# The first load of an elementwise kernel, split by rows into 4 and 60

## Chip, cores, metric

One core of one Trainium2 chip. The metric is the device time of a whole execution in microseconds. Times are medians of several runs; a ratio is the mean time of one kernel's fast runs over the mean of the other's fast runs in the same rounds, so it is not quite the ratio of the medians.

## The reference

```python
B, S, D = 1024, 16, 512          # bf16
def reference(x, y, gamma):      # x, y: (B, S, D); gamma: (D,)
    return x + gamma * y
```

16.8 MB each of x and y are read, and 16.8 MB are written. Seen by 128 partitions, each has 128 rows of 1 KB.

## The kernel before

It is written as lists of transfers. SP loads y and x, ACT loads gamma and stores, VectorE multiplies in place in `y_sb` and then adds x. `x_sb` has room for 75 rows only, so the second x load (rows 64 to 116, the fourth transfer of SP) has to wait for the addition of the first 53 rows. The start barriers are the point at which the engines wait for each other before the program proper; `EARLY` says how many transfers are issued ahead of it.

```python
PIECES = [53, 11, 53, 11]        # rows of one VectorE instruction
SP  = [('y', 0, 64), ('x', 0, 64, 0), ('y', 64, 128), ('x', 64, 117, 0), ('x', 117, 128, 64)]
ACT = [('g',), ('s', 0, 64), ('s', 64, 128)]
EARLY = (1, 0)                   # so many transfers of SP, of ACT, ahead of the start barriers
RELEASE = ('x', 64, 117, 0)      # the stores may start once this load has landed
DVE = [('m', 0), ('m', 1), ('a', 0), ('a', 1), ('m', 2), ('m', 3), ('a', 2), ('a', 3)]
# ... (cut)
            elif kind == "y":
                r = slice(w[1], w[2])
                i = eng.dma_start(out=y_sb[:, r, :], in_=yv[:, r, :]).then_inc(s_load[w], 16)
# ... (cut)
    for kind, *args in DVE:
        c = args[0]
        yt = y_sb[:, starts[c] : starts[c + 1], :]
        if kind == "m":
            need(y_loads, c)     # waits for every y load that meets the piece
            g = gamma_sb[:, None, :].to_broadcast([P, PIECES[c], D])
            nc.vector.tensor_tensor(out=yt, in0=yt, in1=g, op=MULT).then_inc(s_dve, 1)
```

Of the kernel before, what the change touches and what calls it, by code (L numbers as in the profile page):

```python
# [6 lines left out]



SP = [('y', 0, 64), ('x', 0, 64, 0), ('y', 64, 128), ('x', 64, 117, 0), ('x', 117, 128, 64)]  # L10
ACT = [('g',), ('s', 0, 64), ('s', 64, 128)]

EARLY = (1, 0)


RELEASE = ('x', 64, 117, 0)
# [11 lines left out]
def kernel(  # L28
# [30 lines left out]
    y_sb = nc.alloc_sbuf_tensor("y_sb", [P, rows, D], dt).ap()  # L59
    x_loads = [w for w in SP + ACT if w[0] == "x"]  # L60
    y_loads = [w for w in SP + ACT if w[0] == "y"]
    stores = [w for w in SP + ACT if w[0] == "s"]
    for loads in (x_loads, y_loads, stores):
# [32 lines left out]
    def ring(eng, what, n_early):  # L96

        known, went = 0, False
        for k, w in enumerate(what):
            kind = w[0]  # L100
            need = frees(w) if kind == "x" else pieces_of(w[1], w[2]) + list(w[3:]) if kind == "s" else []
            need = max((order[c] + 1 for c in need), default=0)
            if kind == "s" and not went:
                _take(s_go, 1, eng)
                went = True
            if need > known:
                eng.wait_ge(s_add, need)
                known = need
            if kind == "g":
                i = eng.dma_start(out=gamma_row, in_=gamma.unsqueeze(0)).then_inc(s_gamma, 16)  # L110
            elif kind == "x":
                to = x_sb[:, w[3] : w[3] + w[2] - w[1], :]
                i = eng.dma_start(out=to, in_=xv[:, w[1] : w[2], :]).then_inc(s_load[w], 16)
# [3 lines that stand above are left out]
            else:  # L117
                r = slice(w[1], w[2])
                i = eng.dma_start(out=ov[:, r, :], in_=y_sb[:, r, :]).then_inc(s_out, 16)
            if k < n_early:  # L120
                early.append(i.ins)

    ring(nc.sync, SP, EARLY[0])
    ring(nc.scalar, ACT, EARLY[1])

# [84 lines left out]
```

## Time and profile before

| | before |
|---|---|
| time, us (before the change was run) | 120.16 (119.85 to 120.28, 3 runs) |
| span of the profile | 118.6 us |
| VectorE busy | 70.0 us, 59% |
| the two DMA queues | 66.0% + 32.6% of 16 engines |

How to read it: VectorE is idle for two fifths of the span, and the DMA engines for 1.4%. Each DMA engine takes one packet after another; a load gives each of the 16 engines 8 packets and one small packet for the semaphore, the counter by which a waiting engine learns that the data has landed (the 720 packets of q1 are 5 loads of 128 + 16). The lines are in the prediction below. Its packet times come from the trace's record of every DMA packet (start, length, bytes, queue), which the printed page only sums up.

### The profile page before, as it was taken

To read this page: it belongs to the slowest core of one execution; us is meant where nothing else is said; L and a number is where in the kernel's file an instruction comes from. 1 tells how busy PE (TensorE), PEld (TensorE's weight loads), DVE (VectorE), ACT (ScalarE), POOL (GpSimd) and SP (SyncE) were. 2 spreads that over 40 slices of the span, in tenths; PEclk is the share of its full clock that TensorE was granted. 3 is DMA by queue.
4 is the path that set the end of the run, shared out by engine and by line. 5 is a ranking of instruction groups with operands and counts; after the bars stand their busy time and mean duration, and the time that the engine had idled before them with its cause. 6 is when DMAs were issued, how large, how long until landed. Compare 5 with 4: busy or idle time off the path is not lost. (4 is left out here: it accounts for less than half of the span.)

```text
span 118.6 us, 78 instructions
## 1 busy us (share of the span) xinstructions
PE 0.6 (0%) x1; PEld 0.1 (0%) x1; DVE 70.0 (59%) x10; POOL 0.2 (0%) x4
## 2 busy tenths in 40 slices
PE   0001000000000000000000000000000000000000
PEld 0000000000000000000000000000000000000000
DVE  0002000599999299999759999999999910000000
POOL 0000000000000000000000000000000000000000
DMA  9889888998899888998896969598899888988892
GB/s 354 354 376 685 354 354 354 597 464 354 354 398 663 354 354 354 663 398 354 354 586 293 586 293 567 220 639 354 354 575 486 354 354 376 685 354 354 354 619 88
DMA packets 1010, 50.33 MB, mean 424 GB/s; under 512 B 113, under 2 KB 114, under 8 KB 114
## 3 DMA queue, kind: packets, MB, share of 16 engines
q1 hardware_dynamic: 720, 33.55, 66.0%
q10 hardware_dynamic: 290, 16.78, 32.6%
HBM read 33.56 MB, written 16.78 MB: 424 GB/s over the span
## 5 line engine op out<-in xcount | busy, mean ns | idle before, releaser
L156 DVE TENSOR_TENSOR y_sb<-y_sb,gamma_sb 128x27136 bf16<-128x27136 bf16 (+1 forms) x4 | 34.6, 8688 | 12.7 <-DVEq L25 12.7
L165 DVE TENSOR_TENSOR y_sb<-x_sb,y_sb 128x27136 bf16<-128x27136 bf16 (+1 forms) x4 | 34.6, 8688 | 2.3 <-DVEq L25 2.2
L132 DVE CAST gamma_sb<-gamma_ps 128x512 bf16<-128x512 f32 x1 | 0.7, 692 | 8.8 <-DVEq L25 8.8
L127 DVE MEMSET ones_row<- 1x128 bf16 x1 | 0.2, 165 | 1.5 <-PEq L41 1.5
L130 PE MATMUL gamma_ps<-gamma_row,ones_row 1*128 1x512 bf16 x1 | 0.6, 578 | 9.7 <-PEq L25 9.7
L130 PEld LDWEIGHTS gamma_ps<-gamma_row,ones_row 1*128 1x128 bf16 x1 | 0.1, 100 | 9.7 <-issue 9.7
L194 POOL MEMSET const-uint8-127<- 128x1 uint8 x1 | 0.1, 102 | 0.0
L194 POOL MEMSET const-bfloat16-1.0<- 128x1 bf16 x1 | 0.1, 101 | 0.0
L194 POOL MEMSET const-float32-0.0<- 128x1 f32 x1 | 0.1, 98 | 0.2 <-issue 0.2
L194 POOL MEMSET const-float32-1.0<- 128x1 f32 x1 | 0.1, 98 | 0.0
## 6 DMA issues: line engine op xcount, KB each, us to landing
x_sb<-in_x_dram SPq DMA_DIRECT2D x1, 6784.0 KB, 20.8
x_sb<-in_x_dram SPq DMA_DIRECT2D x1, 1408.0 KB, 23.9
y_sb<-in_y_dram SPq DMA_DIRECT2D x2, 40.2
out_dram<-y_sb ACTq DMA_DIRECT2D x2, 22.8
x_sb<-in_x_dram SPq DMA_DIRECT2D x1, 39.7
gamma_row<-in_gamma_dram ACTq DMA_DIRECT2D x1, 1.0 KB
```

The lines of the kernel that those rows point to most:

```text
L127: nc.vector.memset(ones_row, 1.0).then_inc(s_ones, 1)
L130: nc.tensor.matmul(gamma_ps, ones_row, gamma_row, start=True, stop=True).then_inc(s_ps, 1)
L132: nc.vector.tensor_copy(out=gamma_sb, in_=gamma_ps).then_inc(s_dve, 1)
L156: nc.vector.tensor_tensor(out=yt, in0=yt, in1=g, op=MULT).then_inc(s_dve, 1)
L165: nc.vector.tensor_tensor(out=yt, in0=xt, in1=yt, op=ADD).then_inc(s_add, 1)
L194: nc = _bacc.Bacc("TRN2", target_bir_lowering=False, num_devices=1)
```

## The change

The intent is to let a small piece of the first load through first. The 4 rows and the other 60 are two transfers with two semaphores, both ahead of the barriers.

```diff
-SP = [('y', 0, 64), ('x', 0, 64, 0), ('y', 64, 128), ('x', 64, 117, 0), ('x', 117, 128, 64)]
+SP = [('y', 0, 4), ('y', 4, 64), ('x', 0, 64, 0), ('y', 64, 128), ('x', 64, 117, 0), ('x', 117, 128, 64)]
-EARLY = (1, 0)
+EARLY = (2, 0)
```

## The prediction

> **What bounds the kernel now.** I read the engine table first, then the DMA lines of the page, then the waits, then the order of time, and last the single packets in the trace. The page:
>
> ```profile
> span 118.6 us, 78 instructions
> PE 0.6 (0%) x1; PEld 0.1 (0%) x1; DVE 70.0 (59%) x10; POOL 0.2 (0%) x4
> DMA  9889888998899888998896969598899888988892
> ...
> q1 hardware_dynamic: 720, 33.55, 66.0%
> q10 hardware_dynamic: 290, 16.78, 32.6%
> HBM read 33.56 MB, written 16.78 MB: 424 GB/s over the span
> ```
>
> VectorE works 59% of the span, so no compute engine is the bound. The two DMA queues (q1 carries the loads issued by SP, q10 gamma and the stores issued by ACT) together hold 66.0 + 32.6 = 98.6% of the time of the 16 DMA engines. Only 1.4% of 118.6 us, about 1.7 us, is DMA time not filled. The digits of 8 and 9 are not idleness: a packet is counted in the slice in which it starts. Whatever this change does must come out of those 1.7 us, or be added to the rest.
>
> Who waits on the compute side:
>
> ```profile
> DVE y_sb L156 <- DVEq L25: 12.7, 2, 10.8
> DVE gamma_sb L132 <- DVEq L25: 8.8, 1, 8.8
> DVE y_sb L165 <- DVEq L25: 2.2, 1, 2.2
> ```
>
> These are VectorE's waits for loads: 10.8 us for the first y, 2.2 us for x, about 1.9 us for the second y. The data sets the pace. The order of time (start us, length us, what):
>
> ```profile
> 0.00 0.37 SPq L116 DMA_DIRECT2D y_sb<-in_y_dram  x1
> ...
> 1.43 0.33 SPq L113 DMA_DIRECT2D x_sb<-in_x_dram  x1
> 1.43 0.52 ACTq L110 DMA_DIRECT2D gamma_row<-in_gamma_dram  x1
> ...
> 9.70 0.10 PEld L130 LDWEIGHTS gamma_ps<-gamma_row,ones_row 1*128 1x128 bf16 x1 [9.70 <-issue]
> ...
> 10.46 0.69 DVE L132 CAST gamma_sb<-gamma_ps 128x512 bf16<-128x512 f32 x1 [8.78 <-DVEq L25]
> 21.94 17.29 DVE L156 TENSOR_TENSOR y_sb<-y_sb,gamma_sb 128x27136 bf16<-128x27136 bf16 x2 [10.79 <-DVEq L25]
> ...
> 76.88 18.86 ACTq L119 DMA_DIRECT2D out_dram<-y_sb  x2
> ```
>
> The first y load is issued ahead of the start barriers, at 0.00. The other queues start at 1.43, after the barriers. The first multiplication starts at 21.94.
>
> The packet records of the trace complete this. One packet is one partition's contiguous piece: 64 rows are 65,536 B and take 2.418 us when the engine was already busy, which is 27.1 GB/s for an engine and 434 GB/s for 16. Following the records, all 16 engines have a packet in hand at every moment from about 1.6 us to 117.6 us. The first packets start between 1.00 and 1.63 us, take 2.70 to 3.40 us (mean 3.11) and end between 4.04 and 4.55 us. The last engine writes its last semaphore packet at 118.22 us, the first at 117.64. So the span is a start, a stream and a tail:
> - an engine's stream, 40 packets of 2.418, 8 of 2.004 (53 rows) and 8 of 0.42 us (11 rows): 96.7 + 16.0 + 3.4 = 116.1 us;
> - ahead of it, for the last engine, 4.55 - 2.42 = 2.13 us. For a mean engine this is 1.90: about 1.21 until its first packet starts, and 0.69 by which that packet is longer than a warm one;
> - after it about 0.36 us to the end of the span.
>
> 2.13 + 116.1 + 0.36 = 118.6. The time of a run, 120.16, is some 1.5 us more than the span, outside what the change touches.
>
> **What the Trainium skill says.** "DMA: Bandwidth & Descriptors", section "Where 436 GB/s comes from", puts the ceiling of the 16 engines' ports at 435 GB/s; the packets' 434 agree, so the stream is at its ceiling. The same page, section "Latency and other measured facts", gives about 600 ns to the first byte of a DMA issued from SP or ACT. The trace has 0.63 us between the end of the issue (0.37) and the first packet's start (1.00): agreed, if that is what is meant. The page's section "Why a DMA increments its semaphore by 16 and not by 1" says that each engine's last descriptor writes the semaphore; the trace has 16 landings for the first y load, from 21.33 to 21.81 us. "Perfetto Trace Analysis", section "DMA Optimizations", says that splitting DMAs may let some start sooner and helps "If DMA engines are generally idle". Here they are idle only before 1.6 us.
>
> **The change part by part.** In the instruction streams, SP gets one transfer more (4 rows, then 60, both ahead of the barriers), and the first multiplication waits for two semaphores instead of one. Nothing else moves.
>
> 1. More packets. 128 packets of 65,536 B become 128 of 4,096 and 128 of 61,440 B: 8 more for each engine. The fixed part of a packet comes from two sizes: (2004 - 422) ns / (54272 - 11264) B is 36.8 ps a byte, and 422 ns less 11264 x 36.8 ps leaves about 8 ns. 8 x 8 = 64 ns, and one more semaphore packet of 9 ns: about +0.07 us in the stream, fully on the path, since the engines are never idle.
>
> 2. A later barrier. SP's second early issue takes as long as its other issues, 0.33 to 0.45 us, so x and gamma are issued at about 1.85 instead of 1.43. x is not reached in the ring before 20.9 us, so it doesn't count. gamma_sb is ready at about 11.2 us and wanted at 21.94: ten microseconds to spare. It may even land earlier, because it now comes behind short packets instead of 64 KB ones (its 1 KB packet ran at 6.82 us, at the end of a round of large ones). Either way: 0.
>
> 3. The second wait of the multiplication. It still needs all 64 rows, because the piece is 53 rows and the tail of the load comes last. Nothing is multiplied earlier. The semaphore already there is taken within about 0.1 us (21.83 to 21.94 is such a step), and VectorE's lead over the stores (the second store is issued at 95.4, the first one lands until 99.3) absorbs it: 0.
>
> 4. The start. The first transfer has the same 128 descriptors and the same issue, so its first packets should start at the same 1.00 to 1.63 us. Then 8 packets of 158 ns by the fit, 1.26 us in all, cover an engine until about 3.2 us, with the latency of the first. The second transfer, issued some 0.4 us after the first, should have its descriptors there by 1.4 to 2.1 us. So no hole is expected. Whether anything is gained depends on the 0.69 us: a plain latency from the first read to the first write stays as it is with 4 KB.
>
> Sum: +0.07 us if the latency is a constant; 120.16 becomes 120.2.
>
> **The rivals.** *Short packets start faster.* Four cold 8 KB packets of the runtime, before the kernel, took 0.49 to 0.57 us against 0.31 for two others, an excess of about 0.2 to 0.26, not 0.69. If the excess grows with the packet, because something of it is read before the first write, up to 0.69 - 0.24 = 0.45 us is saved: 119.8 with part 1. Against it: 16 engines starting together may be what makes 0.69, and the last engine to start had an excess of only 0.28 with the same 64 KB. I give this one chance in three. *A hole between the two transfers.* If the second transfer's descriptors come late, as a fresh start of about 1 us rather than behind the first, every engine stands still for up to 0.5 us: 120.7. The early issue speaks against it: one in ten. *The early y rows or gamma let VectorE begin earlier.* This would move only VectorE, which is not the bound, and the multiplication needs row 52 anyway: nothing. *A shift in the spread of the engines.* The slowest engine sets the end, and the engines' starts lie 0.5 us apart; another order may move the end by 0.2 us either way.
>
> **Range and chances.** Two parts in three at 120.2, a third at 119.8 with some holes above: 120.1. The three runs of before lie from 119.85 to 120.28 by themselves, and the effects are at most half a microsecond, so 119.6 to 120.5 should hold 8 times in 10. 2% is 2.4 us. A gain of that size is more than the whole 1.7 us of unfilled DMA time, so faster gets 0.01; slower by 2.4 us would need a hole in the stream that nothing in the trace suggests: 0.01.
>
> **What would show it right or wrong.** The profile after should have a span of 118.2 to 118.9 us, q1 with 720 + 128 + 16 = 864 packets, the second multiplication wait without length, VectorE's first multiplication again at about 22 us, and x's issue near 1.85. The first 4 KB packets should start at 1.0 to 1.6; if the latency is constant, the engines pass their first 64 KB at 4.1 to 4.6 as before, and if the first rival is right, at about 3.7 to 4.1. A gap between the end of the eighth short packet and the start of the first 60 KB packet is the second rival. A time outside of the range would mean that the stream itself changed its rate, for instance packets of 61,440 B slower than 2.27 us, or that a later transfer was issued too late.

## The result, and the profile after

120.06 us (119.92 to 120.14, 6 runs) against 120.09 us (119.85 to 120.28, 6 runs). The ratio is 0.9998, 95% interval 0.9985 to 1.0011: no difference that these runs can see, and they would see about 0.16 us. The lines of the page that answer to those of before:

```profile
span 118.7 us, 80 instructions
PE 0.6 (0%) x1; PEld 0.1 (0%) x1; DVE 70.0 (59%) x10; POOL 0.2 (0%) x4
...
q1 hardware_dynamic: 864, 33.55, 66.0%
q10 hardware_dynamic: 290, 16.78, 32.6%
```

q1 has the 864 packets foretold, with the same bytes and the same share of the engines' time. The waits of VectorE (us in total, times, longest):

```profile
DVE y_sb L156 <- DVEq L25: 12.3, 2, 10.3
...
DVE y_sb L165 <- DVEq L25: 2.2, 1, 2.2
```

The first is 0.4 us shorter, only because gamma is ready half a microsecond later and part of the idle time now lies before the second semaphore wait. The order of time shows where the change is and where it ends:

```profile
0.00 0.84 SPq L116 DMA_DIRECT2D y_sb<-in_y_dram  x2
...
1.90 0.33 SPq L113 DMA_DIRECT2D x_sb<-in_x_dram  x1
1.91 0.52 ACTq L110 DMA_DIRECT2D gamma_row<-in_gamma_dram  x1
...
10.21 0.10 PEld L130 LDWEIGHTS gamma_ps<-gamma_row,ones_row 1*128 1x128 bf16 x1 [10.21 <-issue]
...
21.99 17.29 DVE L156 TENSOR_TENSOR y_sb<-y_sb,gamma_sb 128x27136 bf16<-128x27136 bf16 x2 [10.33 <-DVEq L25]
...
76.95 18.85 ACTq L119 DMA_DIRECT2D out_dram<-y_sb  x2
```

SP issues twice in the first 0.84 us, the barriers and gamma come 0.47 us later, and from the first multiplication on (21.99 against 21.94) everything lies 0.05 to 0.07 us later than before.

The packet records at the start, where the prediction left most open:

| | before | after |
|---|---|---|
| an engine's first packet starts, us | 1.00 to 1.63 | 1.00 to 1.25 for 14 engines, 1.82 and 1.83 for two |
| mean length of an engine's first packet | 3.11 us (64 KB) | 0.67 us (4 KB) |
| an engine has its first 64 KB, us | 4.04 to 4.55, mean 4.32 | 4.07 to 4.60, mean 4.32 |
| time lost by a mean engine up to 12 us | 1.89 us | 1.81 us |
| last semaphore packets of the stores | 117.64 to 118.22, mean 117.92 | 117.69 to 118.33, mean 117.95 |

"Time lost" is 12 us less what the packets done by then take at warm lengths (36.8 ps a byte and 8 ns a packet; "warm" is a packet of an engine that has been busy for some microseconds). The end of the first 64 KB is worked out for the change from the end of the first 60 KB packet, less 28 KB at the warm rate. The first 60 KB packets start at 2.78 to 3.38 us, each straight after its engine's last short ones. So there is no hole in this profile. The start shows 0.08 us less lost, the 8 additional packets and the semaphore packet cost less than 0.1 us (see step 1 below), and the end of a mean engine moves by 0.03 us.

### The profile page after: what moved, and what is told of

Read it like the earlier page. It is cut to its first block, busy times and chain, and to the rows that moved or that the text cites. A ratio compares the mean times of both kernels' runs of the same rounds, so it can differ in the third digit from the quotient of the medians.

```text
span 118.7 us, 80 instructions
## 1 busy us (share of the span) xinstructions
PE 0.6 (0%) x1; PEld 0.1 (0%) x1; DVE 70.0 (59%) x10; POOL 0.2 (0%) x4
```

## The experiments

Zero difference can mean that nothing happens or that a gain and a loss cancel. So I tested whether the start and the packets are on the path at all, then took the change apart.

| run | time, us | ratio to before | span of profile | time lost to 12 us |
|---|---|---|---|---|
| late_start | 121.35 | 1.0112 | 120.0 | 3.25 |
| split16 | 122.08 | 1.0167 | 120.1 | 1.86 |
| split32 | 124.31 | 1.0346 | 122.6 | 2.16 |
| use_early | 119.98 | 1.0005 | 118.5 | 1.65 |
| x_early | 120.03 | 0.9995 | 118.6 | 1.86 |
| rest_late | 122.57 | 1.0233 | 120.8 | 3.36 |
| one_row_late | 121.07 | 1.0081 | 119.6 | 2.83 |
| one_row | 120.38 | 1.0030 | 118.9 | 2.01 |
| rest_late8 | 121.01 | 1.0092 | 119.3 | 2.41 |
| rest_late16 | 120.00 | 1.0001 | 118.5 | 1.69 |
| two_rings | 122.26 | 1.0188 | 120.9 | 1.81 |
| two_rings_g | 122.24 | 1.0200 | 120.8 | 1.76 |

The kernel before ran at medians of 119.97 to 120.07 us beside them. All twelve gave correct results.

### late_start: is the start on the path?

```diff
-EARLY = (1, 0)
+EARLY = (0, 0)
```

> The kernel before, with its first load issued after the start barriers instead of ahead of them (no split). Theory A (the start is on the path: 16 engines that never idle after their first packet, so a later first packet moves the end one for one): the first issue moves from 0.00 to about 1.35 us after the point where it was, so about 120.09 + 1.35 = 121.4 us, ratio 1.011. Theory B (a few tenths or more of a late start are caught up later, so nothing at the start can be seen in the time): 120.1 to 120.4, ratio below 1.003.

121.35 us, ratio 1.0112 (1.0099 to 1.0125). Theory A's 121.4 holds. The order of time shows the shift at the issue, at the first multiplication and at the first store:

```profile
1.38 0.36 SPq L116 DMA_DIRECT2D y_sb<-in_y_dram  x1
...
23.35 17.29 DVE L156 TENSOR_TENSOR y_sb<-y_sb,gamma_sb 128x27136 bf16<-128x27136 bf16 x2 [19.16 <-DVEq L25]
...
78.29 18.86 ACTq L119 DMA_DIRECT2D out_dram<-y_sb  x2
```

In before these are 0.00, 21.94 and 76.88. The mean engine loses 1.36 us more at the start, and the span is 1.4 us longer. Nothing is caught up later: a delay of 1.38 us at the start reaches the end whole, within what the runs resolve. That a delay of a tenth does so too was not tested.

### split16 and split32: are the packets on the path?

```diff
-SP = [('y', 0, 64), ...
+SP = [('y', r, r + 4) for r in range(0, 64, 4)] + ...
```

with two of them early; split32 does the same with the x load that follows.

> The change taken fifteen times over: the first 64 rows of y as 16 loads of 4 rows, two of them ahead of the barriers. Theory A (each packet costs about 8 ns beside its bytes and each load one 9 ns semaphore packet with some 6 ns around it on every engine, all of it on the path): 128 x 159 - 8 x 2418 = 1.0 us plus 15 x 15 ns = 0.2 us, so 121.3 us, ratio 1.010. Theory B (the fixed part of a packet is hidden or caught up): 120.1, ratio below 1.003. Theory C (sixteen issues starve the engines): well above 122, with fewer than 16 packets in hand during the first 20 us.

> The same for the first 64 rows of y and the first 64 rows of x, 32 loads of 4 rows. Theory A: twice the cost, +2.4 us, 122.5 us, ratio 1.0205. Theory B: below 120.5. Theory C: above 124.

122.08 us (121.43 to 122.41) and 124.31 us: +2.1 and +4.3 us where A gave +1.2 and +2.4. The cost is on the path, which refutes B, and it grows with the count, but A's size was too small. The profile of split16 is its fastest run, 121.43 us, near A's number. The median 4 KB packet takes 159 ns as fitted in both. But some take 170 to 480 ns (up to 700 in split32): after 4 us, these add 0.5 us to a mean engine in split16 and 1.3 us in split32. The engines' ends also drift apart: the last semaphore packets span 0.58 us in before, 1.06 in split16, 1.59 in split32, and the slowest engine sets the time. C's numbers came out in part for split32 (above 124), but its mechanism did not: between 1.7 and 20 us the records show at most two of the 16 engines without a packet, for less than 0.5 us in all, in either run (gaps of up to 20 ns left aside).

### use_early: would VectorE make something of the early rows?

```diff
-PIECES = [53, 11, 53, 11]
+PIECES = [4, 49, 11, 53, 11]
```

with the multiplications and additions listed accordingly, on top of the change.

> The change, with VectorE made to use the 4 early rows: pieces of 4, 49, 11, 53, 11 rows, so that the first multiplication (4 rows, about 1.1 us) waits only for the first load and for gamma, and can start at about 11.8 us instead of 22. Theory A (VectorE is not the bound): VectorE ends some of its work up to 1 us earlier, the time stays at 120.1, ratio 0.998 to 1.002. Theory D (the split was worth something that VectorE did not take): the first chain ends 1 us earlier and with it the kernel: 119.1, ratio 0.992.

119.98 us, ratio 1.0005 (0.9990 to 1.0019). The order of time shows the piece of 4 rows multiplied ten microseconds earlier:

```profile
11.85 1.23 DVE L156 TENSOR_TENSOR y_sb<-y_sb,gamma_sb 128x2048 bf16<-128x2048 bf16 x1 [0.26 <-DVEq L25]
21.88 16.23 DVE L156 TENSOR_TENSOR y_sb<-y_sb,gamma_sb 128x25088 bf16<-128x25088 bf16 x2 [8.80 <-DVEq L25]
41.35 17.36 DVE L165 TENSOR_TENSOR y_sb<-x_sb,y_sb 128x2048 bf16<-128x2048 bf16 x3 [3.25 <-DVEq L25]
```

The rest of the first half starts at 21.88 as ever, because it waits for the 60 rows. What VectorE gains it hands back in front of the additions: the wait for x grows from 2.2 to 3.25 us, and they start at 41.35 as before (41.39). Theory D falls.

### x_early: what does the later barrier cost by itself?

```diff
-EARLY = (1, 0)
+EARLY = (2, 0)
```

without the split, so that x is the second early transfer.

> The kernel before, unsplit, with its second load (x) also ahead of the barriers: the barrier shift of the change without its split. Theory A (the shift of 0.47 us has slack everywhere): gamma is used at about 10.2 instead of 9.7 us, time 120.1, ratio 0.999 to 1.001. Theory E (the shift costs its 0.4 to 0.5 us and the split gave that back): 120.5, ratio 1.004.

120.03 us, ratio 0.9995 (0.9983 to 1.0006). The shift is free; theory E falls. The zero of the change is not a loss hidden by a gain of that kind.

### rest_late: the split without the second early issue

```diff
-SP = [('y', 0, 64), ('x', 0, 64, 0), ...
+SP = [('y', 0, 4), ('y', 4, 64), ('x', 0, 64, 0), ...
 EARLY = (1, 0)
```

> The split alone: 4 rows ahead of the barriers, the other 60 after them (issue at about 1.43 us). Theory A: the 8 short packets keep an engine busy until 2.8 to 3.4 us, and descriptors of a load issued at 1.43 are there at about 2.4 to 2.7, so no hole: 120.1 to 120.2, ratio 0.999 to 1.002. Theory E: without the barrier shift the split's gain shows: 119.6, ratio 0.996. Theory F (a second load needs its whole start latency again, a hole): 120.5 or more, and first 60 KB packets that start over 0.2 us after the last short ones.

122.57 us (122.15 to 123.76), ratio 1.0233 (1.0199 to 1.0268): 2.5 us slower than before. Theory A failed here, and with it the step that descriptors (the orders from which an engine makes its packets) are there about a microsecond after their issue. The profile is the fastest of the six runs. In the order of time, SP's early issue and the one at 1.43 us are merged into one line:

```profile
0.00 1.76 SPq L116 DMA_DIRECT2D y_sb<-in_y_dram  x2
...
24.11 17.29 DVE L156 TENSOR_TENSOR y_sb<-y_sb,gamma_sb 128x27136 bf16<-128x27136 bf16 x2 [15.26 <-DVEq L25]
43.58 17.29 DVE L165 TENSOR_TENSOR y_sb<-x_sb,y_sb 128x27136 bf16<-128x27136 bf16 x2 [2.17 <-DVEq L25]
```

The first multiplication comes at 24.11 instead of 21.94 us. The wait for x is the 2.17 us of before, so all of the loss lies ahead of it. The packet records show how: the engines end their short packets at 2.60 to 3.10 us. Five have a 60 KB packet in hand by 3.09; the other eleven get theirs only at 4.24 to 5.06 us, 2.8 to 3.6 us after the issue. The 60 KB packets of the first load are also longer than warm ones, by 0.08 us each in the mean and up to about 11 us, so the engines lose time even after the hole. The ends of the engines lie 1.57 us apart instead of 0.58. The mean engine ends 1.77 us later than before, the slowest 2.22 us.

### one_row_late and one_row: is it the hole, and does a short first packet save the start?

```diff
+SP = [('y', 0, 1), ('y', 1, 64), ('x', 0, 64, 0), ...
-EARLY = (1, 0)
+EARLY = (2, 0)        # one_row; one_row_late keeps (1, 0)
```

> One row (1 KB) ahead of the barriers, 63 rows after them. The 8 short packets of an engine last 8 x 46 ns = 0.37 us and end at about 2.3 us; descriptors of the second load come at 2.4 to 2.7 us, and the engines are cold again. Theory A: a hole, 0.3 to 0.9 us on the path, about 120.7, ratio 1.003 to 1.008. Theory G (what counts is only that the engines were woken early; a short hole is caught up): 120.1, ratio below 1.001.

> One row, then 63, both ahead of the barriers. Theory A (the excess of 0.69 us of an engine's first packet is a latency that doesn't depend on the packet's size): first packets of 1 KB take about 0.73 us, 120.1 to 120.2, ratio 0.999 to 1.002. Theory H (the excess grows with the packet's size, so that 1 KB saves most of it): first packets under 0.3 us and 119.6, ratio 0.996.

one_row_late: 121.07 us, ratio 1.0081 (1.0069 to 1.0093), just above A's range. A's hole is there: the short packets are over by 1.34 to 1.69 us (A had 2.3), the 63 KB packets start at 2.37 to 2.91, and they are cold again, 2.91 to 3.29 us against 2.38 warm. The engines' early waking (G) was worth nothing. Here, with idle engines, the load issued at 1.42 did come through after 0.95 us on the first engine and 1.5 us on the last, unlike in rest_late.

one_row: 120.38 us, ratio 1.0030 (1.0013 to 1.0047), slightly slower. Both theories failed in part. The first sixteen 1 KB packets took 0.10 us in the mean, so the excess of 0.69 us is not a latency of whatever packet comes first, as A had it. But nothing was saved, against H: the large packets that followed took 2.5 to 3.4 us, and the excess of a mean engine over warm lengths in its first packets was 0.63 us in total, as against 0.69 in before. Five engines got their first large packet only at 2.02 to 2.38 us, after a short hole. So with first packets of 1, 4 or 64 KB an engine loses about the same in its first few packets. Whether it is bytes or time since the first packet that ends the loss, these runs do not tell apart.

### rest_late8 and rest_late16: how long must the early rows last?

The edit is that of rest_late with 8 and with 16 rows in place of 4.

> As the run with 4 rows ahead of the barriers and the rest after them (which came out 2.5 us slower, with 11 of 16 engines waiting 1.2 to 2.7 us for their first 60 KB packet, although one row alone left a hole of only about 1 us), but with 8 rows ahead: short packets of 8 KB, 309 ns each, keep an engine busy until about 4.4 us. Theory Q (a load issued while the engines stream comes through 2.8 to 4.3 us after its issue at 1.43, so at 4.2 to 5.7): a hole of 0 to 1.3 us, time about 121.0, between 120.4 and 121.8. Theory P (an engine whose first load ends before the next begins always pays the same restart): again about 122.5.

> The same with 16 rows ahead: 16 KB packets, 610 ns each, busy until about 6.8 us. Theory Q: no hole, 120.1 to 120.4, ratio below 1.003. Theory P: again about 122.5.

(The figure of 1.2 to 2.7 us quoted there for rest_late was read too hastily. Eleven starts at 4.24 to 5.06, after ends at 2.60 to 3.10, allow waits of at most 2.5 us.)

121.01 us (120.61 to 121.38), ratio 1.0092, and 120.00 us, ratio 1.0001 (0.9988 to 1.0014). Theory P, a fixed restart, would have given 122.5 twice and falls. Q's numbers are met: with 8 rows, the short packets last until 4.14 to 4.47 us; with 16 until 6.39 to 6.82, and each engine goes straight on to its 48 KB packets. The profile of rest_late8 is of its fastest run and has a hole of only 0.12 us in the mean; the larger part of its loss is packets that last longer than warm ones (0.97 us in an engine's first packets, against 0.69 in before). So a late load is followed by a hole, by slow packets, or both. The landing times of the first halves in the pages of rest_late and of rest_late16, from issue, in us:

```profile
y_sb<-in_y_dram SPq DMA_DIRECT2D x1, 7680.0 KB, 22.6
```

```profile
y_sb<-in_y_dram SPq DMA_DIRECT2D x1, 6144.0 KB, 20.3
```

Both were issued at about 1.43 us, so the first half of y is complete at 24.0 and at 21.7 us, though the two parts together have the same bytes.

### two_rings and two_rings_g: a better start from two queues?

```diff
-SP = [('y', 0, 64), ...           -ACT = [('g',), ('s', 0, 64), ...
+SP = [('y', 0, 32), ...           +ACT = [('y', 32, 64), ('g',), ...     # EARLY = (1, 1)
                                   +ACT = [('g',), ('y', 32, 64), ...     # two_rings_g, EARLY = (1, 2)
```

> An attempt at a better start: rows 0 to 31 of y from SP and rows 32 to 63 from ACT, both ahead of the barriers, gamma behind the latter. If the first packets of an engine waited for the issue of 128 descriptors by one sequencer, two would fill the engines sooner: 119.8. If the start is a latency (as all runs so far say), nothing is won and one more packet row and semaphore cost 0.08 us: 120.1 to 120.3. Gamma then lands only with the second half of y, near 21 us, and the first multiplication starts about 1 us later than in the kernel before, which the 2 us of waiting for x take up.

> The two-ring start with gamma ahead of the second half of y on ACT's queue. In the run before it, gamma landed at 26.5 us instead of 9.6, VectorE fell behind, the third x load was issued at 60.2 instead of 55.7 us, and the engines ran dry for about 1.4 us near 60 us. If that delay is the whole of its 2.3 us, gamma is now used before 5 us, the third x load goes out near 55.7 us and the time is 119.8 to 120.2. If two rings cost something by themselves (packets of 32 KB taken by turns), 120.5 or more with the third x load in time.

122.26 and 122.24 us, ratios 1.0188 and 1.0200. Both expectations failed in the time, and the start was not the reason: the time lost to 12 us is 1.81 and 1.76, like the other early starts. In two_rings gamma came late, and VectorE with it. The order of time around 60 us, two_rings first, then before:

```profile
45.84 17.30 DVE L165 TENSOR_TENSOR y_sb<-x_sb,y_sb 128x27136 bf16<-128x27136 bf16 x2
60.16 0.80 SPq L113 DMA_DIRECT2D x_sb<-in_x_dram  x2
```

```profile
41.39 17.29 DVE L165 TENSOR_TENSOR y_sb<-x_sb,y_sb 128x27136 bf16<-128x27136 bf16 x2 [2.16 <-DVEq L25]
55.71 0.81 SPq L113 DMA_DIRECT2D x_sb<-in_x_dram  x2
```

The second x load (the expectations call it the third) waits for the first additions to free its rows. Issued at 60.16, it comes when the loads ahead of it are used up (y's second half lands by 60.5), and a mean engine stands still for 1.4 us between 58 and 62. In two_rings_g gamma is used at 4.7 us, but the second half of y's first 64 rows, taken by turns with x, lands only at 26.57 us. The first multiplication needs row 52, and so the second x load is late again:

```profile
26.71 17.29 DVE L156 TENSOR_TENSOR y_sb<-y_sb,gamma_sb 128x27136 bf16<-128x27136 bf16 x2 [20.57 <-DVEq L25]
...
58.47 0.80 SPq L113 DMA_DIRECT2D x_sb<-in_x_dram  x2
```

The packet records show where the time goes. The engines end y's second half at 59.64 to 60.14 us in before, at 59.67 to 60.07 in two_rings and at 59.80 to 60.05 in two_rings_g: up to there, two rings cost nothing. In two_rings the late load comes through 0.95 us after its issue, on idle engines, and its first packets are cold again, 0.71 us longer than warm in the mean, as at the start of the kernel. In two_rings_g, issued about 1.5 us before the engines run out, it starts at 59.80 to 60.89 us; the mean hole is 0.25 us, and the first packets are 0.47 us longer than warm. A further 0.25 us lies in the last packets of x (11 KB each), near 78 to 80 us. The engines' ends, 0.25 us apart at 60 us, are 2.2 us apart at the end; why they drift apart there was not tested.

## Why the prediction was right

**The bound.** The prediction said that the DMA stream is never idle and that the start is on the path. late_start shows it: 1.36 us more lost, 1.4 us more span. use_early shows that VectorE's earlier work is handed back.

**Step 1, more packets, +0.07 us.** The lengths came out as fitted: 159 ns at 4 KB and 2.267 us at 60 KB in most packets (fit: 158 and 2268 ns). The sum made of them is too large, though: in the records a packet starts 3 to 4 ns before the one ahead of it ends. Warm 4 KB packets follow each other every 155 ns, and 60 KB ones every 2.264 us. By these steps a further packet costs 4 to 5 ns, not 8, and a semaphore packet 6 ns, so the change about 0.04 us, which is below what the runs resolve. split16 and split32 show that many more packets cost time at the end, but by the same steps the fixed parts are only about 0.6 and 1.3 us of the 2.1 and 4.3 us. The rest goes with packets longer than warm and with the drift of the engines' ends, which the prediction had not counted and whose cause is not shown.

**Step 2, the later barrier, 0.** Shown by x_early. The side remark that gamma may land earlier was wrong: its packet ran at 7.47 instead of 6.82 us.

**Step 3, the second semaphore wait, 0.** The waits and the start of the multiplication agree. That slack is not endless: with the first multiplication at 26.7 and 28.4 us (two_rings_g, two_rings), the second x load was late.

**Step 4, the start.** The first packets started at 1.00 us as foretold (on two engines only at 1.82 and 1.83, later than the 1.63 foretold), and no hole opened. The reason given for that, descriptors about a microsecond after the issue, held in these runs only on idle engines (0.95 us in one_row_late, up to 3.6 us in rest_late). rest_late has the same split with the second issue one microsecond later and loses 2.5 us. The change is safe because both transfers go out ahead of the barriers; the chance of one in ten for a hole was about a smaller hole than the one that a later issue opens.

**The rival of a faster start.** It got one chance in three and up to 0.45 us. In the profile after, 0.08 us less is lost. one_row, with far shorter first packets, is not faster at all. By the test that the prediction itself set, an engine has its first 64 KB at 4.07 to 4.60 us, where the rival asked for 3.7 to 4.1 and a constant loss for 4.1 to 4.6. The rival falls in this size; a gain below 0.16 us can't be excluded. The loss was constant as a sum only: as a latency of whatever packet comes first, it falls (one_row), so for this term the right number came with a reason that did not hold.

What stays open: why a load issued at 1.43 us takes up to 3.6 us to reach engines that stream short packets, and what the 0.6 to 0.7 us of cold time consist of. The traces show when packets start, not what they wait for. No version was faster than before by more than the runs resolve.

## What to carry to other kernels

Here the DMA engines were filled from the second microsecond to the last, and splitting a load only added packets; the time that was left lay at the first and last packets, so look at their records first. If a load is split all the same, the remainder has to be issued long before the first part runs out: here 4 rows covered it with an issue at 0.42 us, while with an issue at 1.43 us 8 were too few and 16 enough. And an idle compute engine is not free of deadlines: it also frees the buffers that later loads wait for.

## What the Trainium skill lacked or had wrong

- "DMA: Bandwidth & Descriptors", section "Latency and other measured facts": about 600 ns to the first byte held for the first load (0.63 us after the issue instruction's end). The entry doesn't cover a load issued while the engines already work on short packets: eleven of 16 engines got theirs 2.5 to 3.3 us after the end of that instruction (rest_late). On idle engines it was 0.62 us again (one_row_late, and the late x load of two_rings).
- "Perfetto Trace Analysis", section "DMA Optimizations": splitting "may allow some to start sooner". It doesn't say that the remainder must be covered: the same split gave ratios of 0.9998 and 1.0233, depending on when the remainder was issued.
- No page that I found gives the cold time of an engine's first packets: 0.6 to 0.7 us beyond warm lengths in most profiles here, about the same with first packets of 1, 4 and 64 KB, and 0.71 us again after a standstill of 1.4 us in the middle of the kernel (two_rings).
